# A decode attention kernel with one more key and one more value buffer, and with its last keys loaded ahead of the last values

## The chip, the cores and the metric

The kernel runs on one core of a Trainium2 chip. The metric is the device time of one execution in microseconds, median of several executions. Each kernel was also run once under the hardware profiler. The span of a profiled run, from first to last instruction, is 1.7 to 1.9 us shorter than the time taken of that same run.

## The reference, cut to what matters

Two decode attentions side by side, one query token and four batches each. A has 32 query heads on 8 key heads and looks at the last 2048 positions; B has 32 heads with a key cache of their own and 8192 positions.

```python
q = (x @ wq).reshape(B, 1, Hq, 128)
p = softmax(einsum("bhqd,bhkd->bhqk", q, k) * 128 ** -0.5)
out = einsum("bhqk,bhkd->bhqd", p, v).reshape(B, 1, Hq * 128) @ wo     # A and B concatenated
```

All in bfloat16. Keys and values are read once: 272 pieces of 2 MiB. With the weights that makes 587 MB.

## The kernel before

The work is cut into 136 chunks, 128 of B (one batch and head each) and then 8 of A (one key head, four batches each). A chunk has 64 blocks of 128 keys, taken in eight groups of eight. SyncE issues all loads in program order, and each waits only for the buffer that it overwrites:

```python
NKB = 3; NVB = 4; NPB = 3; SLAG = 2; PVLAG = 4; NG = 8          # buffers for K, V, P; lags in steps; groups
def dma_k(c):   # waits for the transposes of chunk c - NKB
    waits = [("T", (c - NKB + 1) * NG - 1)] if c >= NKB else []
def dma_v(c):   # waits for the values of chunk c - NVB
    waits = [("pv", c - NVB)] if c >= NVB else []
...
dma_x(1); dma_x(0); dma_wq(1); dma_k(0)
for c in range(NC):                      # load order
    if c + 1 < NC:
        dma_k(c + 1)
    dma_v(c)
    ...                                  # wq of A after c == 4, output weights when a chunk needs them
```

TensorE runs one static order, made of steps. In step s it transposes group s ("tr"), multiplies group s - 2 with the query ("sc"), and multiplies one group of an earlier chunk's values with its probabilities ("po"):

```python
for s in range(NC * NG):
    when(s, 0, lambda s=s: emit_T(s))                 # transposes; VectorE or ScalarE copies them out
    when(s + SLAG, 2, lambda s=s: emit_S(s))          # scores
for c in range(NC):
    s0 = c * NG + NG - 1 + SLAG
    when(s0, 3, ...stats_rowmax)                      # maximum: VectorE, TensorE (two small ones), VectorE
    when(s0 + 1, 1, ...stats_gmax)
    when(s0 + 2, 1, ...stats_exp)                     # exponentials on ScalarE, their sums on VectorE (A)
    for g in range(NG):
        when(s0 + PVLAG + g, 4, ...emit_pv)           # values
    if ch["ab"] == 0 or ch["b"] == NB - 1:
        when(s0 + PVLAG + 2, 1, ...norm_sum)          # TensorE adds the sums over the partitions
        when(s0 + PVLAG + NG - 1, 5, ...norm_out)     # VectorE divides: oT
        when(s0 + PVLAG + NG, 3, ...emit_fin)         # output projection: "fin"
```

In all timelines below an engine takes its instructions in this order, and where one waits, those behind it wait too.

Of the kernel before, what the change touches and what calls it, by code (L numbers as in the profile page):

```python
# [9 lines left out]
BF16 = mybir.dt.bfloat16  # L10
F32 = mybir.dt.float32

P = 128
TG = 8
NTRB = 3
NKT = 4
NKB = 3
NVB = 4
NWO = 4
NPB = 3  # L20
NSM = 4
SLAG = 2
NW = 64
PVLAG = 4
# [47 lines left out]
def bass_concat_heads__sliding_block_cached__mha_block_cached__decode_kernel(nc, A_x, A_k, A_v, A_wq, A_wo, B_x, B_k, B_v, B_wq, B_wo, out):  # L72
    NB = A_x.shape[0]
# [3 lines left out]
    HQ = A_wq.shape[1] // P  # L77
# [3 lines left out]
    KC = D // P  # L81
# [4 lines left out]
    NT = JB  # L86
    NG = NT // TG
    scale = 1.0 / math.sqrt(P)
    X = {0: A_x, 1: B_x}
    WQ = {0: A_wq, 1: B_wq}  # L90
# [8 lines left out]
    NC = len(chunks)  # L99
    wo_list = []  # L100
    for c, ch in enumerate(chunks):
# [3 lines left out]
        wo_list[-1][2] = c  # L105
        ch["wo_i"] = len(wo_list) - 1
    NBC = HB * NB

    sch = _Sched()
    with ExitStack() as es:  # L110
        block = es.enter_context(nc.Block())

        def sb(name, shape, dt):
            return es.enter_context(nc.sbuf_tensor(name, shape, dt))
# [3 lines left out]

        kn = sb("kn", [P, NKB, NT * P], BF16)
        vn = sb("vn", [P, NVB, NT * P], BF16)  # L120
        kt = sb("kt", [P, NKT, TG * P], BF16)
        wqr = sb("wqr", [P, KC * HQ * P], BF16)
        wor = sb("wor", [P, NWO, 4 * DO], BF16)
        xs = sb("xs", [NB, 2, D], BF16)
        xT = sb("xT", [P, 2, KC * NB], BF16)
# [12 lines left out]
        tmp = sb("tmp", [P, 2, 256], F32)  # L138
        pb = sb("pb", [P, NPB, 256 + NW], BF16)
        oT = sb("oT", [P, NSM, 16], BF16)  # L140
# [7 lines left out]

        semnames = ["eng_pe", "eng_dve", "eng_act", "eng_pool", "d_x0", "d_x1", "d_o0", "d_o1"]
        semnames += ["d_k%d" % i for i in range(NKB)] + ["d_v%d" % i for i in range(NVB)]  # L150
        semnames += ["d_wq%d" % i for i in range(2)] + ["d_wo%d" % i for i in range(NWO)]
        sems = {n: es.enter_context(nc.semaphore(n)) for n in semnames}


# [11 lines left out]


        def dma_x(ab):
            sch.add_dma("sp", lambda e: e.dma_start(xs[:, ab, :], X[ab][:, 0, :]), "d_x%d" % ab, key=("x", ab))

        def dma_wq(ab):

            n = KC // 2 * HQ * P
            for i in range(2):
                src = WQ[ab].rearrange("(p r) n -> p (r n)", r=KC)[:, i * n:(i + 1) * n]
                waits = [("qmm", 1)] if ab == 0 else []
                sch.add_dma("sp", lambda e, i=i, src=src: e.dma_start(wqr[:, i * n:(i + 1) * n], src),
                            "d_wq%d" % i, waits=waits, key=("wq", ab, i))

        def dma_wo(i):  # L180
            (ab, wg), _, _ = wo_list[i]
            slot = i % NWO
            src = WO[ab][wg * 4 * P:(wg + 1) * 4 * P, :].rearrange("(hl d) n -> d hl n", d=P)
            dst = wor[:, slot, :].rearrange("p (hl n) -> p hl n", hl=4)
            waits = [("fin", wo_list[i - NWO][2])] if i >= NWO else []
            sch.add_dma("sp", lambda e: e.dma_start(dst, src), "d_wo%d" % slot, waits=waits, key=("wo", i))

        def kv_src(T, ch):
            if ch["ab"] == 1:
                return T[ch["b"], ch["h"]].rearrange("(p j) d -> p (j d)", p=P)  # L190
            return T[:, ch["g"], SkA - W:, :].rearrange("b (p j) d -> p b (j d)", p=P)

        def kv_dst(buf, slot, ch):
            d = buf[:, slot, :]
            return d if ch["ab"] == 1 else d.rearrange("p (b x) -> p b x", b=NB)

        def dma_k(c):
            ch = chunks[c]
            src, dst = kv_src(A_k if ch["ab"] == 0 else B_k, ch), kv_dst(kn, c % NKB, ch)
            waits = [("T", (c - NKB + 1) * NG - 1)] if c >= NKB else []  # L200
            sch.add_dma("sp", lambda e: e.dma_start(dst, src), "d_k%d" % (c % NKB), waits=waits, key=("k", c))  # L201

        def dma_v(c):
            ch = chunks[c]
            src, dst = kv_src(A_v if ch["ab"] == 0 else B_v, ch), kv_dst(vn, c % NVB, ch)
            waits = [("pv", c - NVB)] if c >= NVB else []
            sch.add_dma("sp", lambda e: e.dma_start(dst, src), "d_v%d" % (c % NVB), waits=waits, key=("v", c))

        dma_x(1)
        dma_x(0)  # L210
        dma_wq(1)
        dma_k(0)
        wo_next = 0
        for c in range(NC):
            if c + 1 < NC:
                dma_k(c + 1)
            dma_v(c)
            if c == 4:
                dma_wq(0)
            while wo_next < len(wo_list) and wo_list[wo_next][1] <= c:  # L220
                dma_wo(wo_next)
                wo_next += 1


        ms_read = []
        po_read = []
# [14 lines left out]
        def emit_q(ab):  # L241
            for h in range(HQ):
                for r in range(KC):
                    o = ms[:, Q0 + h * NB: Q0 + (h + 1) * NB]
                    l = wqr[:, (r * HQ + h) * P:(r * HQ + h + 1) * P]
                    rr = xT[:, ab, r * NB:(r + 1) * NB]
                    last = h == HQ - 1 and r == KC - 1
                    sch.add("pe", lambda e, o=o, l=l, rr=rr, r=r: e.matmul(o, l, rr, start=(r == 0), stop=(r == KC - 1)),  # L248
                            waits=[("wq", ab, 0), ("wq", ab, 1), "xT"] + ([("q", 1)] if ab == 0 else []) + ms_read if h == r == 0 else [],
                            key=("qmm", ab) if last else None)  # L250
            src = ms[:, Q0:Q0 + HQ * NB].rearrange("p (h b) -> p h b", b=NB)
            dst = qs[:, ab * NB * HQ:(ab + 1) * NB * HQ].rearrange("p (b h) -> p h b", b=NB)
            sch.add("dve", lambda e: e.tensor_copy(dst, src), waits=[("qmm", ab), "c_qs"], key=("q", ab))
            ms_read[:] = [("q", ab)]


        def emit_T(s):
            c, g = divmod(s, NG)
            bank = s % NTRB
            for t in range(TG):  # L260
                o = tr[:, bank, t * P:(t + 1) * P]
                i_ = kn[:, c % NKB, (g * TG + t) * P:(g * TG + t + 1) * P]
                waits = []
# [59 lines left out]
        def stats_exp(c):  # L323
# [6 lines left out]
            ms_read[:] = [("negb", c)]  # L330
            pbv = pb[:, c % NPB, 0:NT * C]
            pw = [("pv", c - NPB)] if c >= NPB else []
            if n == 1:
# [29 lines left out]
        def emit_pv(c, g):  # L363
            ch = chunks[c]
            C, J = ch["C"], ch["J"]
            for t in range(TG):
                j = g * TG + t
                u, jj = divmod(j, J)
                base = norm_slot(c)[2] * 16 + (ch["b"] if ch["ab"] == 1 else u * C)
                o = po[:, base:base + NW]  # L370
                l = vn[:, c % NVB, j * P:(j + 1) * P]
                r = pb[:, c % NPB, j * C:j * C + NW]
                waits = [("v", c), "c_pb", ("exp", c)] + po_read if g == 0 and t == 0 else []
                sch.add("pe", lambda e, o=o, l=l, r=r, jj=jj: e.matmul(o, l, r, start=(jj == 0), stop=(jj == J - 1)),  # L374
                        waits=waits, key=("pv", c) if j == NT - 1 else None)

# [8 lines left out]
        def norm_out(c):  # L385
            m, n, s = norm_slot(c)
            sch.add("dve", lambda e: e.tensor_tensor(out=oT[:, m, 0:n], in0=po[:, s * 16:s * 16 + n], in1=rinv[:, m, 0:n], op=ALU.mult),  # L387
                    waits=[("rinv", c), ("pv", c)], key=("oT", c))
            po_read[:] = [("oT", c)]

        def emit_fin(c):
# [5 lines left out]
            else:  # L397
                ov = oT[:, m, 0:n].rearrange("p (u c) -> p u c", c=REP)
                ops = [(fin[32:32 + NB, :], ov[:, :, cc], w[:, cc, :]) for cc in range(REP)]
            lastc = NBC - 1 if ch["ab"] == 1 else NC - 1  # L400
            for i, (o, l, r) in enumerate(ops):
# [15 lines left out]
        def when(s, prio, fn):  # L417
            at.setdefault(s, []).append((prio, len(at.get(s, [])), fn))
# [4 lines left out]
        for c in range(NC):  # L423
            ch = chunks[c]
            s0 = c * NG + NG - 1 + SLAG
            when(s0, 3, lambda c=c: stats_rowmax(c))
            when(s0 + 1, 1, lambda c=c: stats_gmax(c))
            when(s0 + 2, 1, lambda c=c: stats_exp(c))
            for g in range(NG):
                when(s0 + PVLAG + g, 4, lambda c=c, g=g: emit_pv(c, g))  # L430
            if ch["ab"] == 0 or ch["b"] == NB - 1:
                when(s0 + PVLAG + 2, 1, lambda c=c: norm_sum(c))
                when(s0 + PVLAG + NG - 1, 5, lambda c=c: norm_out(c))
                when(s0 + PVLAG + NG, 3, lambda c=c: emit_fin(c))
        when(8 * NG, 5, lambda: emit_q(0))

        emit_xT()
        emit_q(1)
# [53 lines left out]
```

## Time and profile before

| | before |
|---|---|
| time, median of 3 | 1432.7 us (1432.53 to 1433.11) |
| span of the profiled run | 1431.4 us |
| TensorE busy, transfer engines busy | 83%, 9 tenths or more in 39 of 40 slices |
| last key chunk, last transfer, end | 1408.4, 1422.7, 1431.4 us |

The prediction below shows lines of the profile's page and reads them. Its times of landing do not stand on the page. The trace records sixteen semaphore updates for a transfer; "a chunk lands" means the sixteenth, and the spread is the time from the first to the sixteenth. The record of an update names no transfer engine. That each of the sixteen is one engine's, so that early and late updates are early and late engines, is the author's reading.

### The profile page before, as it was taken

Reading aid. Unit: us, or ns where it says so; the run is one execution under the profiler, and the core shown is the slowest. Engines: PE = TensorE matmul, PEld = TensorE weight load, DVE = VectorE, ACT = ScalarE, POOL = GpSimd, SP = SyncE. Lnnn points to the kernel's source line nnn. Section 1 sums busy time; section 2 is a strip of 40 time slices with the busy share of each in tenths; the row PEclk is TensorE's granted clock in tenths of the full one; section 3 lists DMA queues with packets and bytes.
Section 4 is the critical chain, followed back from the end, with each engine's and each line's share of the span. In section 5 each row is a group of like instructions: output and inputs, shape, how many; then the busy total and the mean of one; then the engine's idle time right before and its main releaser. Section 6 shows DMA issues by size and latency. Waiting matters only on the chain.

```text
span 1431.4 us, 56275 instructions
## 1 busy us (share of the span) xinstructions
PE 1195.2 (83%) x26928; PEld 1128.4 (79%) x26928; DVE 590.4 (41%) x1267; ACT 422.3 (30%) x627; POOL 2.4 (0%) x11
## 2 busy tenths in 40 slices
PE   5969888988888878888888888888888887888887
PEld 4858887887888877878778878787787787878776
DVE  2423443444444434444443434444434343444444
ACT  1312332332232322323323323333223232323221
POOL 0000000000000000000000000000000000000000
PEclk9988999999999999999999999999999999999999
DMA  9999999999999999999999999999999999999996
GB/s 389 425 426 426 425 422 422 426 424 424 423 422 424 422 422 420 410 422 416 423 412 424 416 419 407 424 418 421 423 407 425 419 418 415 419 418 406 370 395 244
DMA packets 54596, 590.83 MB, mean 413 GB/s; under 512 B 4688, under 2 KB 12896, under 8 KB 21088
## 3 DMA queue, kind: packets, MB, share of 16 engines
q1 hardware_dynamic: 54368, 587.24, 98.2%
q8 instruction: 211, 3.46, 1.0%
q14 instruction: 17, 0.14, 0.0%
HBM read 587.21 MB, written 0.01 MB: 410 GB/s over the span
## 4 chain that ended last, share of the span: by engine, by line
DMA 69%; PE 28%; issue 1%; DVE 1%; SPq 0%; ACT 0%; DVEq 0%
DMA kn<-in_B_k_cache_dram 56%; PE tr L266 13%; DMA vn<-in_B_v_cache_dram 8%; PE sc L295 7%; PE po L374 6%; DMA kn<-in_A_k_cache_dram 6%; PE ms L327 1%; PE ms L313 1%; PE fin L404 0%; PE ms L248 0%; DVE kt L273 0%; SPq L201 0%; PE ms L380 0%; DVE tmp L346 0%; DVE rm L307 0%
## 5 line engine op out<-in xcount | busy, mean ns | idle before, releaser
L266 PE MATMUL tr<-identb,kn 128*128 128x128 bf16 x8704 | 687.5, 223 | 196.1 <-DMA kn<-in_B_k_cache_dram 172.7
L273 DVE COPY kt<-tr 128x1024 bf16<-128x1024 bf16 x726 | 502.2, 692 | 714.2 <-PE tr L266 710.3
L266 PEld LDWEIGHTS tr<-identb,kn 128*128 128x128 bf16 x8704 | 520.0, 100 | 212.7 <-DMA kn<-in_B_k_cache_dram 186.1
L271 ACT ACTIVATE kt<-tr 128x1024 bf16<-128x1024 bf16 x362 | 370.7, 1024 | 857.2 <-PE tr L266 851.6
L295 PE MATMUL sc<-qs,kt 128*128 128x64 bf16 x8704 | 452.3, 195 | 7.3 <-issue 7.2
L374 PE MATMUL po<-pb,vn 128*128 128x64 bf16 x8704 | 449.4, 195 | 9.9 <-issue 7.4
L295 PEld LDWEIGHTS sc<-qs,kt 128*128 128x128 bf16 x8704 | 376.8, 100 | 13.4 <-issue 9.0
L374 PEld LDWEIGHTS po<-pb,vn 128*128 128x128 bf16 x8704 | 342.3, 99 | 22.9 <-issue 18.4
L335 ACT ACTIVATE pb<-sc,negb 128x64 bf16<-128x64 f32 x128 | 40.0, 312 | 126.2 <-DVE negb L329 126.2
L327 PE MATMUL ms<-gm,nsc 1*128 1x1 f32 x256 | 48.5, 256 | 0.8 <-issue 0.8
L327 PEld LDWEIGHTS ms<-gm,nsc 1*128 1x128 f32 x256 | 37.7, 183 | 13.6 <-issue 0.2
L315 DVE TENSOR_REDUCE gm<-ms 1x1 f32<-1x128 f32 (+1 forms) x136 | 37.0, 272 | 20.2 <-PE ms L313 20.2
L307 DVE TENSOR_REDUCE rm<-sc 128x1 f32<-128x64 f32 (+1 forms) x136 | 31.3, 230 | 29.7 <-PE sc L295 29.4
L313 PE MATMUL ms<-identf,rm 128*1 128x128 f32 (+1 forms) x136 | 38.3, 282 | 1.3 <-DVE rm L307 1.3
L329 DVE COPY negb<-ms 128x1 f32<-128x1 f32 (+1 forms) x136 | 20.8, 153 | 27.8 <-PE ms L327 27.8
L335 ACT ACTIVATION_READ_ACCUMULATOR pb<-sc,negb 128x1 f32 x128 | 25.1, 196 | 0.0
L404 PE MATMUL fin<-wor,oT 128*4 128x512 bf16 x64 | 20.3, 378 | 4.1 <-DVE oT L387 4.1
L313 PEld LDWEIGHTS ms<-identf,rm 128*1 128x1 f32 (+1 forms) x136 | 11.5, 85 | 13.5 <-DVE rm L307 13.4
L248 PE MATMUL ms<-xT,wqr 128*128 128x4 bf16 x256 | 7.0, 166 | 10.9 <-DMA wqr<-in_B_wq_dram 10.9
L248 PEld LDWEIGHTS ms<-xT,wqr 128*128 128x128 bf16 x256 | 6.9, 102 | 10.9 <-issue 10.9
L380 PE MATMUL ms<-rs,onesf 128*128 128x4 f32 (+1 forms) x80 | 13.6, 241 | 0.0
L380 PEld LDWEIGHTS ms<-rs,onesf 128*128 128x128 f32 x80 | 12.1, 191 | 0.0
(26 smaller groups left out, 45.3 us busy)
## 6 DMA issues: line engine op xcount, KB each, us to landing
kn<-in_B_k_cache_dram SPq DMA_DIRECT2D x128, 2048.0 KB, 22.5
vn<-in_B_v_cache_dram SPq DMA_DIRECT2D x128, 2048.0 KB, 27.1
kn<-in_A_k_cache_dram SPq DMA_DIRECT2D x8, 2048.0 KB, 21.3
vn<-in_A_v_cache_dram SPq DMA_DIRECT2D x8, 2048.0 KB, 21.5
wqr<-in_B_wq_dram SPq DMA_DIRECT2D x2, 2048.0 KB, 9.6
wor<-in_B_wo_dram SPq DMA_DIRECT2D x8, 512.0 KB, 28.1
wqr<-in_A_wq_dram SPq DMA_DIRECT2D x2, 2048.0 KB, 32.8
wor<-in_A_wo_dram SPq DMA_DIRECT2D x8, 512.0 KB, 17.4
```

What stands on the lines that cost most here:

```text
L266: sch.add("pe", lambda e, o=o, i_=i_: e.transpose(o, i_, identb[:, :]), waits=waits, key=("T", s) if t == TG - 1 else None)
L271: sch.add("act", lambda e: e.activation(dst, src, ACTF.Copy), waits=waits, key=("ev", s))
L273: sch.add("dve", lambda e: e.tensor_copy(dst, src), waits=waits, key=("ev", s))
L295: sch.add("pe", lambda e, o=o, l=l, q=q: e.matmul(o, l, q, start=True, stop=True), waits=waits, key=("S", s) if t == TG - 1 else None)
L307: sch.add("dve", lambda e: e.tensor_reduce(out=dst, in_=src, axis=AX.X, op=ALU.max), waits=[("S", (c + 1) * NG - 1)], key=("rowmax", c))
L313: sch.add("pe", lambda e: e.transpose(ms[0:n, col:col + P], rm[:, m, 0:n], identf[:, :]), waits=[("rowmax", c), "c_identf"] + ms_read, key ...
L315: sch.add("dve", lambda e: e.tensor_reduce(out=gm[0:n, m, :], in_=ms[0:n, col:col + P], axis=AX.X, op=ALU.max), waits=[("trm", c)], key=(" ...
L327: sch.add("pe", lambda e: e.matmul(ms[:, col:col + n], nsc[0:n, :], rhs, start=True, stop=True), waits=[("dg", c) if n > 1 else ("gmax", c ...
L329: sch.add("dve", lambda e: e.tensor_copy(negb[:, m, 0:n], ms[:, col:col + n]), waits=[("bc", c)], key=("negb", c))
L335: sch.add("act", lambda e: e.activation(pbv, sc[:, c % 2, 0:NT], ACTF.Exp, bias=negb[:, m, 0:1], scale=scale, accum_out=ri), waits=[("negb ...
L374: sch.add("pe", lambda e, o=o, l=l, r=r, jj=jj: e.matmul(o, l, r, start=(jj == 0), stop=(jj == J - 1)), waits=waits, key=("pv", c) if j == ...
L380: sch.add("pe", lambda e: e.matmul(ms[:, col:col + n], onesf[:, :], rs[:, m, 0:n], start=True, stop=True), waits=[("rs", c), "c_onesf"] + ...
```

## The change

Its intent: keep more transfers under way, and end the kernel with less work behind the last transfer. The query weights, 32 KB a partition, now lie in value buffers that are not yet in use, and the room pays for one more buffer each for keys and values. All keys are loaded ahead of the last three value chunks (133, 134, 135), so that only values are left to do when the last bytes land, and the last value chunk comes as four transfers, each with its own semaphore. The core of the diff:

```diff
-NKB = 3
-NVB = 4
+NKB = 4
+NVB = 5
-NPB = 3
+NPB = 4
-        wqr = sb("wqr", [P, KC * HQ * P], BF16)
+        wqr = {1: vn[:, 0:2, :].rearrange("p s x -> p (s x)"), 0: vn[:, 2:4, :].rearrange("p s x -> p (s x)")}
@@ x loads: issued by ScalarE instead of SyncE
-            sch.add_dma("sp", ... xs[:, ab, :] ...)
+            sch.add_dma("act", ... xs[:, ab, :] ...)
@@ dma_v
-            waits = [("pv", c - NVB)] if c >= NVB else []
+            waits = [("pv", c - NVB)] if c >= NVB else ([("qmm", 1 - slot // 2)] if slot < 4 else [])
+            if c == NC - 1:
+                for u in range(NB):
+                    sch.add_dma("sp", ... dst[:, u, :], src[:, u, :] ..., "d_vl%d" % u, ...)
+                return
@@ load order
+        loads = [("k", c + 1) for c in range(NC - 1)]
+        for c in range(NC):
+            loads.insert(min(2 * c + 1, NC - 1 + c) if c < NC - 3 else len(loads), ("v", c))
@@ order of TensorE
+            v0 = s0 + PVLAG if c < NC - 3 else (NC - 1) * NG + NG - 1 + SLAG + PVLAG + (c - NC + 1) * NG + 2 * NG
-                when(s0 + PVLAG + g, 4, lambda c=c, g=g: emit_pv(c, g))
+                when(v0 + g, 4, lambda c=c, g=g: emit_pv(c, g))
-                when(s0 + PVLAG + NG - 1, 5, lambda c=c: norm_out(c))
-                when(s0 + PVLAG + NG, 3, lambda c=c: emit_fin(c))
+                when(v0 + NG - 1, 5, lambda c=c: norm_out(c))
+                when(v0 + NG, 3, lambda c=c: emit_fin(c))
```

(A's query weights are loaded at the start, the second query matmuls move from step 64 to step 5, and output weights are loaded one chunk earlier.) The values of chunks 133, 134 and 135 now follow, one after the other, all transposes and scores.

More of the change, by code (lines that the diff above doesn't have):

```diff
@@ L107, in bass_concat_heads__sliding_block_cached__mha_block_cached__decode_kernel @@
     NBC = HB * NB
+    assert KC * HQ == 2 * NT
     sch = _Sched()
@@ L150, in bass_concat_heads__sliding_block_cached__mha_block_cached__decode_kernel @@
         semnames += ["d_k%d" % i for i in range(NKB)] + ["d_v%d" % i for i in range(NVB)]
-        semnames += ["d_wq%d" % i for i in range(2)] + ["d_wo%d" % i for i in range(NWO)]
+        semnames += ["d_wq0", "d_wq1"] + ["d_vl%d" % i for i in range(NB)] + ["d_wo%d" % i for i in range(NWO)]
         sems = {n: es.enter_context(nc.semaphore(n)) for n in semnames}
@@ L168, in dma_x @@
         def dma_x(ab):
-            sch.add_dma("sp", lambda e: e.dma_start(xs[:, ab, :], X[ab][:, 0, :]), "d_x%d" % ab, key=("x", ab))
+            sch.add_dma("act", lambda e: e.dma_start(xs[:, ab, :], X[ab][:, 0, :]), "d_x%d" % ab, key=("x", ab))
+        wqr = {1: vn[:, 0:2, :].rearrange("p s x -> p (s x)"), 0: vn[:, 2:4, :].rearrange("p s x -> p (s x)")}
         def dma_wq(ab):
-            n = KC // 2 * HQ * P
-            for i in range(2):
-                src = WQ[ab].rearrange("(p r) n -> p (r n)", r=KC)[:, i * n:(i + 1) * n]
-                waits = [("qmm", 1)] if ab == 0 else []
-                sch.add_dma("sp", lambda e, i=i, src=src: e.dma_start(wqr[:, i * n:(i + 1) * n], src),
-                            "d_wq%d" % i, waits=waits, key=("wq", ab, i))
+            src = WQ[ab].rearrange("(p r) n -> p (r n)", r=KC)
+            sch.add_dma("sp", lambda e: e.dma_start(wqr[ab], src), "d_wq%d" % ab, key=("wq", ab))
         def dma_wo(i):
@@ L204, in dma_v @@
             ch = chunks[c]
-            src, dst = kv_src(A_v if ch["ab"] == 0 else B_v, ch), kv_dst(vn, c % NVB, ch)
-            waits = [("pv", c - NVB)] if c >= NVB else []
-            sch.add_dma("sp", lambda e: e.dma_start(dst, src), "d_v%d" % (c % NVB), waits=waits, key=("v", c))
+            slot = c % NVB
+            src, dst = kv_src(A_v if ch["ab"] == 0 else B_v, ch), kv_dst(vn, slot, ch)
+            waits = [("pv", c - NVB)] if c >= NVB else ([("qmm", 1 - slot // 2)] if slot < 4 else [])
+            if c == NC - 1:
+                for u in range(NB):
+                    sch.add_dma("sp", lambda e, u=u: e.dma_start(dst[:, u, :], src[:, u, :]), "d_vl%d" % u, waits=waits, key=("vl", u))
+                return
+            sch.add_dma("sp", lambda e: e.dma_start(dst, src), "d_v%d" % slot, waits=waits, key=("v", c))
         dma_x(1)
@@ L212, in bass_concat_heads__sliding_block_cached__mha_block_cached__decode_kernel @@
         dma_k(0)
+        dma_wq(0)
+        loads = [("k", c + 1) for c in range(NC - 1)]
+        for c in range(NC):
+            loads.insert(min(2 * c + 1, NC - 1 + c) if c < NC - 3 else len(loads), ("v", c))
         wo_next = 0
-        for c in range(NC):
-            if c + 1 < NC:
-                dma_k(c + 1)
-            dma_v(c)
-            if c == 4:
-                dma_wq(0)
-            while wo_next < len(wo_list) and wo_list[wo_next][1] <= c:
-                dma_wo(wo_next)
-                wo_next += 1
+        for kind, c in loads:
+            (dma_k if kind == "k" else dma_v)(c)
+            if kind == "v":
+                while wo_next < len(wo_list) and wo_list[wo_next][1] <= c + 1:
+                    dma_wo(wo_next)
+                    wo_next += 1
         ms_read = []
@@ L244, in emit_q @@
                     o = ms[:, Q0 + h * NB: Q0 + (h + 1) * NB]
-                    l = wqr[:, (r * HQ + h) * P:(r * HQ + h + 1) * P]
+                    l = wqr[ab][:, (r * HQ + h) * P:(r * HQ + h + 1) * P]
                     rr = xT[:, ab, r * NB:(r + 1) * NB]
@@ L248, in emit_q @@
                     sch.add("pe", lambda e, o=o, l=l, rr=rr, r=r: e.matmul(o, l, rr, start=(r == 0), stop=(r == KC - 1)),
-                            waits=[("wq", ab, 0), ("wq", ab, 1), "xT"] + ([("q", 1)] if ab == 0 else []) + ms_read if h == r == 0 else [],
+                            waits=[("wq", ab), "xT"] + ([("q", 1)] if ab == 0 else []) + ms_read if h == r == 0 else [],
                             key=("qmm", ab) if last else None)
@@ L372, in emit_pv @@
                 r = pb[:, c % NPB, j * C:j * C + NW]
-                waits = [("v", c), "c_pb", ("exp", c)] + po_read if g == 0 and t == 0 else []
+                waits = ["c_pb", ("exp", c)] + po_read if g == 0 and t == 0 else []
+                if c == NC - 1:
+                    waits += [("vl", u)] if jj == 0 else []
+                elif j == 0:
+                    waits += [("v", c)]
                 sch.add("pe", lambda e, o=o, l=l, r=r, jj=jj: e.matmul(o, l, r, start=(jj == 0), stop=(jj == J - 1)),
@@ L428, in bass_concat_heads__sliding_block_cached__mha_block_cached__decode_kernel @@
             when(s0 + 2, 1, lambda c=c: stats_exp(c))
+            v0 = s0 + PVLAG if c < NC - 3 else (NC - 1) * NG + NG - 1 + SLAG + PVLAG + (c - NC + 1) * NG + 2 * NG
             for g in range(NG):
-                when(s0 + PVLAG + g, 4, lambda c=c, g=g: emit_pv(c, g))
+                when(v0 + g, 4, lambda c=c, g=g: emit_pv(c, g))
             if ch["ab"] == 0 or ch["b"] == NB - 1:
                 when(s0 + PVLAG + 2, 1, lambda c=c: norm_sum(c))
-                when(s0 + PVLAG + NG - 1, 5, lambda c=c: norm_out(c))
-                when(s0 + PVLAG + NG, 3, lambda c=c: emit_fin(c))
-        when(8 * NG, 5, lambda: emit_q(0))
+                when(v0 + NG - 1, 5, lambda c=c: norm_out(c))
+                when(v0 + NG, 3, lambda c=c: emit_fin(c))
+        when(5, 5, lambda: emit_q(0))
         emit_xT()
```

## The prediction

Its sum came to 1429.6 us for the span and 1430.9 for the time. What the trace of before does show: after 460 us the largest gap among a transfer's sixteen updates lies behind the eighth, in all 172 transfers of B; and the clock is at half in 21 stretches of 3.4 to 13.7 us, the last from 1409.3 for 3.4, behind the wait of 2.14 us for key 135. That the 24 long steps are the fetches of q8, and that eight engines share these, is an estimate from the page's count and share.

> **What bounds the kernel now.** I read the page's DMA part first, then the chain of waits, then the single transfers' landings, and last the TensorE timeline of the final 35 us.
>
> ```profile
> DMA  9999999999999999999999999999999999999996
> GB/s 389 425 426 426 425 422 422 426 424 424 423 422 424 422 422 420 410 422 416 423 412 424 416 419 407 424 418 421 423 407 425 419 418 415 419 418 406 370 395 244
> ...
> q1 hardware_dynamic: 54368, 587.24, 98.2%
> q8 instruction: 211, 3.46, 1.0%
> ...
> DMA 69%; PE 28%; issue 1%; DVE 1%; SPq 0%; ACT 0%; DVEq 0%
> ```
>
> The transfer engines are busy in every slice but the last, and the chain that ended last is 69% transfers: the kernel streams 587 MB and TensorE (83% busy[...]) follows. The change moves the same bytes, so the first question is whether the 410, 407 and 370 GB/s slices are lost time that more buffers could win back.
>
> They look like it. In this view of two stretches (busy times of the engines, then the granted clock, the DMA share and GB/s) a hole can be seen:
>
> ```profile
> 573.00:577.00 4.00, 4.00 (x108) 4.00 (x104) 1.98 (x3) 1.02 (x1) 0.00 (x0) 1.00 0.74 291
> 577.00:584.00 7.00, 6.08 (x145) 5.66 (x142) 3.35 (x8) 2.45 (x4) 0.00 (x0) 1.00 0.99 412
> ```
>
> But the trace also records each of the sixteen semaphore updates of every transfer[...]. Sorted by time they say something else. The spread from first to last of the sixteen is 0.5 us for the first keys (18.2 to 18.7 us), 8 us near 270 us, 14 us near 450 us, and then stays at 14 to 16 us to the end of the B stage. Always about eight engines are early and eight late. And the last of the sixteen lands at 574.6, 579.6, 584.4, 589.3, 594.2 us straight across the hole: a step of 4.9 us for each 2 MiB, as in the fullest slices. **The late engines never pause; only the early ones do**, because they have used up all that the buffers let be issued. Of the 253 steps of the last update between 50 and 1305 us, nearly all are 4.9 us (or 1.5 for an output-weight load), and 24 are 6.4 us. The q8 row explains those 24: 211 instruction fetches, 1.0% of 16 engines' 1431 us, so 1.1 us each; 211 over eight engines is 26 each. The slowest engine therefore needs 246 steps of 4.89 us, 7 of 1.5 and 24 extras of 1.5, together 1250 us, and took 1251. It has no idle time to give back.
>
> Now the end. Rows are start, duration, engine, line, operation, and in brackets the idle time and its releaser:
>
> ```profile
> 1385.06 0.62 PE L266 MATMUL tr<-identb,kn 128*128 128x128 bf16 x8 [1.29 <-DMA kn<-in_A_k_cache_dram]
> ...
> 1396.76 0.62 PE L266 MATMUL tr<-identb,kn 128*128 128x128 bf16 x8 [1.65 <-DMA kn<-in_A_k_cache_dram]
> ...
> 1408.44 0.62 PE L266 MATMUL tr<-identb,kn 128*128 128x128 bf16 x8 [2.14 <-DMA kn<-in_A_k_cache_dram]
> ...
> 1422.11 0.39 PE L327 MATMUL ms<-dg,nsc 16*128 16x16 f32 x2 [0.40 <-DVE dg L319]
> 1422.43 0.64 PE L374 MATMUL po<-pb,vn 128*128 128x64 bf16 x16
> 1424.40 1.03 PE L404 MATMUL fin<-wor,oT 128*4 128x512 bf16 x4 [1.33 <-DVE oT L387]
> ...
> 1427.96 1.03 PE L404 MATMUL fin<-wor,oT 128*4 128x512 bf16 x4 [0.34 <-DVE oT L387]
> ```
>
> The last three key chunks (133, 134, 135) arrive at 1385.0, 1396.7 and 1408.4. The last value chunk has landed at 1421.4 and the last output weights at 1422.7 (sixteenth updates), yet the span ends at 1431.4: from 1408.4 on it is a TensorE chain of 23.0 us, which outlives the last transfer by 8.7 us.
>
> [...] the x loads moved to ScalarE's queue are worth what they held up: the first weight load is issued at 1.53 us, behind two x issues that start at 0.81. [...] the clock is 0.79 in 1408 to 1416.
>
> **The change part by part.**
>
> 1. Query weights in the value buffers. 32 KB a partition come free and pay for one more K and one more V buffer of 16 KB. New waits: V0 and V1 wait for the first query matmuls (done near 18 us), V2 and V3 for the second. Issued ahead of those are 4+2+4+2 MiB, which at 424 GB/s keep the engines busy to some 32 us, and then K2, K3, V0, V1 to some 50 us. The second query matmuls wait for weights landing near 29 us, so they end near 34 us: no hole. Cost 0.
>
> 2. One more buffer each. The early eight engines may run some 10 us further ahead; the late eight gain nothing, by the working above. Worth 0. The holes should shrink all the same.
>
> 3. x on the other queue: everything lands 1.53 - 0.81 = 0.7 us earlier. NPB 4 changes nothing: its wait is on work long done.
>
> 4. Keys ahead. Each output-weight load goes one chunk earlier. Key 134 comes after the same bytes as before plus one such load (1.45 us) minus 0.7: 1396.7 + 0.75 = 1397.5. Key 135 follows 5.1 us later, at 1402.6, not at 1408.4. All loads still end near 1422.7 - 0.7 = 1422.0, now with the last V piece.
>
> TensorE from there, every piece from the rows of before: chunk 134's eight groups took 9.4 us warm (1396.76 to 1406.2) with eight value groups of 0.235 us in between; three of these leave for later, so 8.7, to 1406.2. Then chunk 135 at once, without any value groups (8 x 0.235) and without an output projection (0.96): 9.4 - 2.84 = 6.6, so 1412.8. Its last score matmuls start 1.57 us after the last transposes' start (1418.72 to 1420.29), thus near 1413.9; 1.8 us on (to 1422.11) comes the broadcast of the maximum, 1415.7, and 0.32 later the postponed values of chunk 133, at 1416.05. After two of their groups stands the sum over chunk 135's exponentials, in program order, and those are ready 2.16 us after the broadcast (1422.11 to 1424.27): **a new wait of about 1.4 us**, to 1417.9. Sum 0.2, six groups 1.4, normalization gap 0.32: projection of 133 at 1419.9. Then twice (0.96 projection, 1.88 values, 0.32 gap): projection of 134 at 1423.05, of 135 at 1426.2. From there to the end it was 1431.38 - 1427.96 = 3.42 us. End: 1429.6, that is 1.8 us less. The last V piece (1422.0) is there before TensorE comes to chunk 135's values (1424.0), so cutting it in pieces is worth nothing yet.
>
> The timed figure is 1.3 us above the profiled span (1432.7 against 1431.4): 1430.9.
>
> **The rivals.**
>
> - The end is set by the last transfer: TensorE catches up. Then 1422.0 + 16 matmuls (0.5) + 0.3 + 3.42 = 1426.2, timed 1427.5. For it: the diff is built for this. Against: the sum above, 3.4 us longer.
> - The stream itself gets faster through the buffers. At 426 GB/s throughout, 590.8 MB need 1387 us, the end would be near 1400, 2% less. For it: the holes. Against: the unbroken 4.9 us steps of the sixteenth updates.
> - A cold clock in the new tail. Waiting for key 134 (some 1.7 us) or in the new 1.4 us wait the clock may halve for 3 to 4 us: plus 1.5 to 2, so 1432.7, no gain. For it: 0.79 in 1408 to 1416 before. Against: chunk 135 now follows 134 without a wait.
> - A fetch falls late on the slowest engine: plus or minus 1.5 us on the last landings, hidden where TensorE is the bound.
>
> **Range and chances.** Some 0.55 for the main sum (1430.9), 0.25 for something near the transfer bound (1428), 0.15 for the cold clock (1432.7), little for the stream. Mean 1430.4, said as 1430.5; range 1427.3 to 1433.0. Two per cent is 28.7 us, over three times all that lies after the last landing (8.7), so only the stream rival could reach it: 0.02 faster, 0.01 slower.
>
> **What would show it.** Sixteenth updates in B still 4.9 us apart with some 24 long steps, their spread growing to some 25 us: step 2 right. Key 135 landing near 1402.6, last landing near 1422.0: step 4. TensorE waiting for ScalarE's or VectorE's sum of chunk 135 near 1417, no wait on V pieces, end near 1429.6: the tail. The prediction is wrong if the last landing moves by more than 3 us, or if TensorE waits for the last V piece.

## The result, and the profile after

The changed kernel took **1434.15 us** (1433.66 to 1434.8, 4 runs); the kernel before, in the same rounds, 1432.89. The ratio is 1.0009, with a 95% interval of 0.9992 to 1.0027: the same. A ratio here and below is the mean time of one kernel's runs over the mean of the other's of the same rounds, so not quite the ratio of the medians quoted. The prediction was 1430.5, and 1434.15 lies above its range (to 1433.0). The profiled run took 1434.55, with a span of 1432.8.

The page of the changed kernel, the lines that answer to those shown of before (the share of transfers in the chain last):

```profile
DMA  9999999999999999999999999999999999998995
GB/s 401 422 425 424 424 423 425 424 427 420 425 424 425 424 423 424 426 425 422 422 426 424 408 416 423 425 424 393 423 426 422 414 411 426 422 419 345 367 398 223
...
q1 hardware_dynamic: 54112, 587.23, 97.9%
q8 instruction: 211, 3.46, 1.0%
...
DMA 79%; PE 19%; DVE 1%; issue 0%; SPq 0%; ACT 0%; DVEq 0%
```

The stream as a whole has not moved: the same 587 MB and the same 211 instruction fetches; slices 37 and 38, where A begins, are at 345 and 367 GB/s, for 406 and 370 before. Yet the buffers do what they were made for. From the list of transfers, with the size of one and the median time from issue to landing, first of before, then of the changed kernel:

```profile
kn<-in_B_k_cache_dram SPq DMA_DIRECT2D x128, 2048.0 KB, 22.5
vn<-in_B_v_cache_dram SPq DMA_DIRECT2D x128, 2048.0 KB, 27.1
```

```profile
kn<-in_B_k_cache_dram SPq DMA_DIRECT2D x128, 2048.0 KB, 32.4
vn<-in_B_v_cache_dram SPq DMA_DIRECT2D x128, 2048.0 KB, 36.9
```

Each chunk is asked for 10 us earlier and lands when it did. For the end, the TensorE timeline of the changed kernel from the maximum of chunk 135 on (L320 and L334), to be compared with the last rows of before in the prediction:

```profile
1415.39 0.28 PE L320 MATMUL ms<-identf,rm 128*16 128x128 f32 x1 [0.52 <-DVE rm L314]
1416.30 0.39 PE L334 MATMUL ms<-dg,nsc 16*128 16x16 f32 x2 [0.63 <-DVE dg L326]
1416.62 0.80 PE L385 MATMUL po<-pb,vn 128*128 128x64 bf16 x16
1418.51 0.61 PE L391 MATMUL ms<-rs,onesf 128*128 128x16 f32 x2 [1.09 <-DVE rs L360]
1418.96 2.72 PE L385 MATMUL po<-pb,vn 128*128 128x64 bf16 x48
1421.95 1.87 PE L415 MATMUL fin<-wor,oT 128*4 128x512 bf16 x4 [0.27 <-DVE oT L398]
1423.75 2.04 PE L385 MATMUL po<-pb,vn 128*128 128x64 bf16 x64
1426.06 1.03 PE L415 MATMUL fin<-wor,oT 128*4 128x512 bf16 x4 [0.27 <-DVE oT L398]
1427.01 2.04 PE L385 MATMUL po<-pb,vn 128*128 128x64 bf16 x64
1429.39 1.03 PE L415 MATMUL fin<-wor,oT 128*4 128x512 bf16 x4 [0.34 <-DVE oT L398]
```

The wait of 1.09 us for the sum of chunk 135 (L391) is new. The values of chunk 135 start at 1427.01, with no transfer in the brackets: the last of them had landed at 1422.2, so the four pieces were of no use. And the same work takes two different times: 48 value matmuls take 2.72 us at 1418.96, where before they took 1.56, and four projections 1.87 us at 1421.95, but 1.03 at 1426.06. The row of before:

```profile
1426.06 1.56 PE L374 MATMUL po<-pb,vn 128*128 128x64 bf16 x48
```

That is the clock. Stretches of the changed kernel's run (busy time of each engine with its count, then the granted clock, the DMA share, GB/s):

```profile
1406.00:1414.00 8.00, 7.03 (x149) 6.52 (x147) 5.98 (x17) 3.42 (x4) 0.00 (x0) 1.00 1.01 386
1414.00:1418.00 4.00, 2.15 (x39) 1.53 (x35) 2.29 (x10) 0.41 (x1) 0.00 (x0) 0.87 0.52 204
1418.00:1424.00 6.00, 5.22 (x63) 3.61 (x64) 0.85 (x3) 0.00 (x1) 0.00 (x0) 0.52 0.18 74
1424.00:1432.80 8.80, 5.81 (x134) 4.11 (x130) 1.03 (x3) 0.00 (x0) 0.00 (x0) 1.00 0.01 2
```

TensorE is busy for only 2.15 of the 4 us from 1414 on, and has half its clock, by the trace's record, from 1416.9 for 6.8 us.

Step by step, by the prediction's own list:

| | predicted us | measured us |
|---|---|---|
| spread of the sixteen updates, end of B | some 25 | 22.6 to 24.2 |
| key 134, key 135 land | 1397.5, 1402.6 | 1397.7, 1402.8 |
| last transfer lands | 1422.0 | 1422.2 |
| transposes of 135 begin | 1406.2 | 1406.4 |
| values of 133 begin | 1416.05 | 1416.6 |
| new wait for the sum ends | 1417.9 | 1418.5 |
| projection of 133 | 1419.9 | 1421.95 |
| projection of 134 | 1423.05 | 1426.06 |
| projection of 135 | 1426.2 | 1429.39 |
| end | 1429.6 | 1432.8 |

### The profile page after: what moved, and what is told of

It is laid out like the page before. It is cut to its first block, busy times and chain, and to the rows that moved or that the text cites. A ratio compares the mean times of both kernels' runs of the same rounds, so it can differ in the third digit from the quotient of the medians. Undisturbed runs are those within 1.5% of the kernel's fastest.

```text
span 1432.8 us, 56273 instructions
## 1 busy us (share of the span) xinstructions
PE 1203.7 (84%) x26928; PEld 1133.7 (79%) x26928; DVE 590.2 (41%) x1267; ACT 421.8 (29%) x627; POOL 2.7 (0%) x11
## 4 chain that ended last, share of the span: by engine, by line
DMA 79%; PE 19%; DVE 1%; issue 0%; SPq 0%; ACT 0%; DVEq 0%
DMA kn<-in_B_k_cache_dram 66%; PE tr L273 9%; DMA kn<-in_A_k_cache_dram 7%; DMA vn<-in_B_v_cache_dram 5%; PE po L385 4%; PE sc L302 4%; DMA vn<-in_A_wq_dram 2%; PE ms L334 1%; PE ms L320 0%; DVE kt L280 0%; PE fin L415 0%; PE ms L255 0%; PE ms L391 0%; DVE rm L314 0%; DVE tmp L353 0%
## 5 line engine op out<-in xcount | busy, mean ns | idle before, releaser
L334 PE MATMUL ms<-gm,nsc 1*128 1x1 f32 x256 | 48.5, 256 | 0.5 <-issue 0.4
L334 PEld LDWEIGHTS ms<-gm,nsc 1*128 1x128 f32 x256 | 37.5, 182 | 14.1 <-issue 0.5
L320 PE MATMUL ms<-identf,rm 128*1 128x128 f32 (+1 forms) x136 | 38.4, 282 | 1.6 <-DVE rm L314 1.6
L320 PEld LDWEIGHTS ms<-identf,rm 128*1 128x1 f32 (+1 forms) x136 | 11.6, 85 | 13.5 <-DVE rm L314 13.4
L255 PE MATMUL ms<-xT,vn 128*128 128x4 bf16 x256 | 7.1, 166 | 10.4 <-DMA vn<-in_A_wq_dram 6.0
L398 DVE TENSOR_TENSOR oT<-po,rinv 128x4 bf16<-128x4 f32 (+1 forms) x40 | 6.3, 158 | 21.9 <-PE po L385 21.9
L255 PEld LDWEIGHTS ms<-xT,vn 128*128 128x128 bf16 x256 | 7.0, 104 | 10.6 <-DMA vn<-in_A_wq_dram 6.1
L391 PE MATMUL ms<-rs,onesf 128*128 128x4 f32 (+1 forms) x80 | 13.8, 244 | 1.1 <-DVE rs L360 1.1
```

The source lines that it names most:

```text
L320: sch.add("pe", lambda e: e.transpose(ms[0:n, col:col + P], rm[:, m, 0:n], identf[:, :]), waits=[("rowmax", c), "c_identf"] + ms_read, key ...
L334: sch.add("pe", lambda e: e.matmul(ms[:, col:col + n], nsc[0:n, :], rhs, start=True, stop=True), waits=[("dg", c) if n > 1 else ("gmax", c ...
```

## The experiments

**Theory.** The stream ends when its slowest transfer engine does, and the buffers can't hurry that engine. The tail after the last key is one chain on TensorE. The change cut the wait for keys from it but laid the values of three chunks behind it, and made pauses (0.52, 0.63 and 1.09 us), around which the clock fell to half for 6.8 us. **Rivals.** Either deeper buffers do win time in the stream and the tail loses it again; or the last transfer sets the end, and no order on TensorE matters. Four runs come first.

### Only the buffers

Buffers, query weights and x loads as in the change; load order, TensorE order and whole last values as before.

```diff
-            loads.insert(min(2 * c + 1, NC - 1 + c) if c < NC - 3 else len(loads), ("v", c))
+            loads.insert(min(2 * c + 1, NC - 1 + c), ("v", c))
-            v0 = s0 + PVLAG if c < NC - 3 else (NC - 1) * NG + NG - 1 + SLAG + PVLAG + (c - NC + 1) * NG + 2 * NG
+            v0 = s0 + PVLAG
```

> Only the new buffers (query weights in the value buffers, 4 K, 5 V, 4 P buffers, x on the other queue); load order, value groups and whole last V as before the change. Theory (the eight late transfer engines never pause, buffers win nothing): 1432.2 us, the 0.7 us of the earlier start and no more; sixteenth landings in B still 1251 us for the same 253 steps. Rival (the holes in the DMA rate were lost time that deeper buffers win back): 1405 to 1428 us.

Measured: 1432.3 us (1431.44 to 1432.94, 5 runs) beside 1432.53; ratio 0.9997 (0.9983 to 1.001). The 253 steps of the sixteenth update in B took 1250.8 us, against 1251.2 before, while the median key landed 32.5 us after its issue instead of 22.5. The rival that buffers win time in the stream falls. Whether the 0.7 us of the start are there can't be told from times that scatter by 1.5 us; the last landing is at 1421.7 instead of 1422.7.

### The sum later

```diff
-                when(s0 + PVLAG + 2, 1, lambda c=c: norm_sum(c))
+                when(s0 + PVLAG + 2 if c < NC - 1 else v0 + 2, 1, lambda c=c: norm_sum(c))
```

> The changed kernel with the sum over chunk 135's exponentials moved from between the values of chunk 133 to after two groups of chunk 135's values. Theory (the tail is one TensorE chain, lengthened by the 1.1 us wait for this sum and by the half clock that follows the pauses): 1.1 us less for the wait, 1433.0, and some 2.5 us less again if the clock stays full because TensorE no longer pauses, 1430.5. Rival (the last transfer sets the end): 1434.1, no change.

Measured: 1430.68 us (1430.16 to 1432.56, 5 runs); ratio to before 0.9988 (0.9976 to 1.0001). The last transfer lands at 1422.1, as in the changed kernel, and every run is faster than every run of the changed kernel, so the rival that it sets the end falls. The clock did fall, at 1417.4, but for 3.4 us instead of 6.8. The profiled span was 1430.8, 2.0 us less than the changed kernel's: more than the wait alone (1.1), less than wait and clock together.

### Transposes that nobody reads, in the pauses

Eight before L320, ten before L334, sixteen before L391 (`e0` is the step of chunk 135's maximum):

```diff
+        def fill(n):
+            for i in range(n):
+                o = tr[:, 2, (i % TG) * P:(i % TG + 1) * P]
+                sch.add("pe", lambda e, o=o: e.transpose(o, identb[:, :], identb[:, :]), waits=[("ev", NC * NG - 3)])
+        when(e0 + 1, 0, lambda: fill(8)); when(e0 + 2, 0, lambda: fill(10)); when(e0 + PVLAG + 2, 0, lambda: fill(16))
```

> The changed kernel with 34 transposes of the identity, whose result nobody reads, put where TensorE waits in the tail (8 before the transposed maximum, 10 before the broadcast, 16 before the sum). No wait is removed. Theory (the half clock from 1417 to 1424 us costs 2.6 us and comes of the pauses): the clock stays full, 1431.5. Rival (the clock is not what costs, or it falls for another reason): 1434 or a little more.

Measured: 1432.12 us (1431.63 to 1434.55, 5 runs); ratio to before 0.9999 (0.9986 to 1.0011). The TensorE timeline of this run (L451 are the added ones):

```profile
1414.97 0.61 PE L451 MATMUL tr<-identb 128*128 128x128 bf16 x8
...
1417.36 1.06 PE L451 MATMUL tr<-identb 128*128 128x128 bf16 x16
1418.77 0.40 PE L391 MATMUL ms<-rs,onesf 128*128 128x16 f32 x2 [0.35 <-DVE rs L360]
1419.01 1.56 PE L385 MATMUL po<-pb,vn 128*128 128x64 bf16 x48
1420.84 1.03 PE L415 MATMUL fin<-wor,oT 128*4 128x512 bf16 x4 [0.27 <-DVE oT L398]
```

The sum comes no earlier (1418.77 against 1418.51), but the 48 value matmuls take 1.56 us instead of 2.72 and the projections 1.03 instead of 1.87. Adding useless work took about 2 us off this tail. From the start of the broadcast (L334) to the end it is 14.3 us here. In the four profiles of the tail without these transposes it is 16.5, 16.7 and 16.8 us where the clock was halved for 6.8 us (the changed kernel, and the runs with one whole last value chunk and with eight engines, below), and 15.7 where it was halved for 3.4 (the changed kernel again, below). By the medians the gain is of that size too, but their intervals overlap; the profiles are what shows it.

When did the clock fall? In the records of before and of the changed kernel every stretch within the span, at full clock or at half, lasts 3.41 us or a multiple of it, up to 13.65 at half clock. Windows here are these 3.4 us. TensorE's busy time in the window ahead of the fall was 2.1 us in the changed kernel and 2.1 in the run with the later sum; with the added transposes it was 3.1 in the same stretch, and the clock stayed. In none of these does TensorE pause for more than 0.63 us at once. But busy time does not tell the cases apart: in the run with the buffers alone TensorE is busy for 2.1 us of the window from 1421.6 too, and the clock stays full. What does is the number of columns that the matmuls which start in the window stream (128 for a transpose, 64 for a score or value matmul, 512 for a projection): 2416 in the changed kernel and 2720 with the later sum, against 4736 with the transposes and 3744 with the buffers alone. Counted over all 14 profiles, from 41 us on and without the last windows of each, 5347 windows had the full clock and 315 of them were followed by half of it. None of the 315 had more than 3200 columns, and none of the others fewer than 2888. Of the windows with 1.5 to 2.14 us of busy time, 26 were followed by a fall and 615 were not.

### The values of chunk 133 between

If pauses cost, useful work belongs in them. The values of 133 have landed at 1407.9, and the transposes of 135 begin at 1406.4.

```diff
-            v0 = s0 + PVLAG if c < NC - 3 else (NC - 1) * NG + NG - 1 + SLAG + PVLAG + (c - NC + 1) * NG + 2 * NG
+            v0 = s0 + PVLAG if c < NC - 3 else (NC - 1) * NG + 4 + (c - NC + 3) * NG
```

(The sum of 135 as in "The sum later".)

> The changed kernel with the values of chunk 133 put between the last transposes and scores of chunk 135 and into its waits, 134 and 135 directly after, and the sum of 135 inside its own values. Theory (the end is a TensorE chain whose waits can hold work): about 4 us off the chain, with a full clock a span near 1427.5, timed 1429; the last V piece (1422.2) just begins to matter. Rival (the last transfer sets the end): no change, 1434.

Measured: 1431.95 us (1430.74 to 1432.99, 5 runs); ratio 0.9994 (0.9981 to 1.0006). A miss, and the timeline shows why:

```profile
1416.68 0.41 PE L385 MATMUL po<-pb,vn 128*128 128x64 bf16 x8
1418.64 1.87 PE L415 MATMUL fin<-wor,oT 128*4 128x512 bf16 x4 [1.56 <-DVE oT L398]
```

The projection of 133 waits 1.56 us for its normalization (oT), although the values of 133 are done at 1417.1. The last group of those values stands in the same step as the statistics of 135, so VectorE has the sum over 135's exponentials in its queue first, and that waits for ScalarE. The clock fell again, from 1418.1 for 3.4 us.

### One step earlier

```diff
-            v0 = s0 + PVLAG if c < NC - 3 else (NC - 1) * NG + 4 + (c - NC + 3) * NG
+            v0 = s0 + PVLAG if c < NC - 3 else (NC - 1) * NG + 3 + (c - NC + 3) * NG
```

In VectorE's order the division for 133 now comes ahead of the statistics of 135. This run was sent with three others; first the changed kernel again, unaltered, then the same with one whole last value chunk.

> The changed kernel unaltered, on the chip of this job, to see how far two runs of one kernel differ. Theory (its tail ends about 10.5 us after the last landing, whether or not a half-clock window of 3.4 or 6.8 us falls on it): 1431 to 1435 us, last landing near 1422.2. Rival (it is truly slower than before in some other place): the last landing later than before's 1422.7.

```diff
-            if c == NC - 1:
+            if False:                                         # the last value chunk loaded whole
-                if c == NC - 1:
-                    waits += [("vl", u)] if jj == 0 else []
-                elif j == 0:
+                if j == 0:                                    # and waited for whole
                     waits += [("v", c)]
```

> The changed kernel with the last value chunk loaded whole and waited for whole. Theory (the last V has landed before TensorE comes to it): the same as the changed kernel beside it within 1 us, and no wait on a V transfer in the tail. Rival (the pieces let TensorE start on the last V early): 1.4 us more, and TensorE waits for V.

> The values of chunk 133 one step earlier than in the run values_between, so that VectorE's normalization of 133 stands before the exponential statistics of 135 in its queue; the rest as there. Theory (in values_between the projection of 133 waited 1.56 us because its normalization stood behind ScalarE's exponentials in VectorE's order): that wait goes, values of 135 start near 1420.8, ahead of the last V piece at 1422.1, and the last transfer sets the end: span 1426.5 to 1427.5, timed 1428 to 1429. Rival (another wait takes its place): span 1430, timed 1431.5.

Measured beside 1432.7 for the kernel before:

| | time us | range (5 runs) | ratio to before, 95% | span of the profiled run |
|---|---|---|---|---|
| changed, again | 1434.4 | 1433.39 to 1436.16 | 1.0012 (1.0000 to 1.0024) | 1431.6 |
| one whole last V | 1434.93 | 1433.62 to 1434.97 | 1.0013 (1.0001 to 1.0024) | 1433.2 |
| values one step earlier | 1429.46 | 1428.54 to 1430.32 | 0.9976 (0.9964 to 0.9988) | 1426.7 |

The changed kernel repeats, and its clock falls again in both profiles of the first two rows (at 1417.8 for 3.4 us, at 1417.6 for 6.8), which would account for most of the 1.6 us between their spans. In pieces or whole makes no difference to it. The third beats the kernel before, by 0.24%, and the changed one. Its timeline:

```profile
1416.16 0.39 PE L334 MATMUL ms<-dg,nsc 16*128 16x16 f32 x2 [0.40 <-DVE dg L326]
1416.48 1.03 PE L415 MATMUL fin<-wor,oT 128*4 128x512 bf16 x4
1417.44 2.04 PE L385 MATMUL po<-pb,vn 128*128 128x64 bf16 x64
1419.74 1.03 PE L415 MATMUL fin<-wor,oT 128*4 128x512 bf16 x4 [0.27 <-DVE oT L398]
1420.70 0.64 PE L385 MATMUL po<-pb,vn 128*128 128x64 bf16 x16
1421.18 0.37 PE L391 MATMUL ms<-rs,onesf 128*128 128x16 f32 x2
1421.40 1.56 PE L385 MATMUL po<-pb,vn 128*128 128x64 bf16 x48
1423.30 1.03 PE L415 MATMUL fin<-wor,oT 128*4 128x512 bf16 x4 [0.34 <-DVE oT L398]
```

The broadcast of the maximum (L334) is where it was in the changed kernel, 1416.2 against 1416.3. But the projection of 133 follows at once, and the projection of 135 starts 6.1 us earlier. All at full clock: 4896 columns in the 3.4 us from 1413.6. The last landing is 1421.8 and the end 4.9 us later. But no line waits for a value transfer: TensorE comes to the last piece, the last 16 of these 64 value matmuls, at 1422.3, 0.5 us after it landed. So even here the last transfer does not set the end: that part of the expectation did not come true, though little is missing.

### The last value chunk, where TensorE arrives early

```diff
-            if c == NC - 1:
-                for u in range(NB): ...
+            # the last value chunk as any other, in the kernel "values one step earlier"
```

> The kernel of values_earlier with the last value chunk in one piece. Theory (there TensorE comes to the last values at 1420.7, before the last landing at 1421.8, so here the pieces do count): TensorE waits for V some 1.1 us, values of 135 from 1422.0, span 1427.8 against 1426.7, timed 1 us more than values_earlier. Rival (pieces are worth nothing here either): the same time.

Measured: 1430.19 us (1429.88 to 1431.39, 5 runs), ratio to before 0.9984 (0.9972 to 0.9997), span 1428.1. The line that decides:

```profile
1422.12 0.63 PE L383 MATMUL po<-pb,vn 128*128 128x64 bf16 x16 [0.26 <-DMA vn<-in_A_v_cache_dram]
```

Now TensorE waits for values. The wait is only 0.26 us because in this run the projection of 134 came 1.1 us later (1420.84 against 1419.74). So the span is 1.4 us longer than with pieces, but this trace puts down only that wait to the missing pieces; the rest came earlier in the run, and the profiled run with pieces was the fastest of its five. By the ratios the pieces are worth 1.1 us, with overlapping intervals.

### Transposes that nobody reads, in the best kernel

```diff
+        when(e0 + 1, 0, lambda: fill(5)); when(e0 + 2, 0, lambda: fill(6))      # fill as above
```

> The kernel of values_earlier with 11 transposes of the identity, read by nobody, in the two pauses before chunk 135's maximum. Theory (in values_earlier the clock was full through the tail already): no change in the profiled run, 1429.5, and a narrower scatter if the clock fell in some of its unprofiled runs. Rival (the clock falls in many runs): up to 1.5 us less.

Measured: 1429.38 us (1428.68 to 1430.17, 5 runs), ratio 0.9977 (0.9965 to 0.999), clock full through the tail. No change, as expected: there was no fall left to prevent.

### What sets the stream

> The kernel of the run values_earlier plus 12288 one-element memsets on GpSimd, which has nothing else to do after 4 us. They move no data through the transfer queues but are 64 bytes each to fetch, 0.79 MB or 48 fetches of 16 KB more than the 211. Theory (instruction fetches delay eight of the sixteen transfer engines by 1.5 us each, and the slowest engine sets the stream): 6 more per late engine, last landing 9 us later, near 1431, time near 1438.5. Rival (fetches fill holes of the queue, or land on early engines): 1429.5, no change.

```diff
+        for i in range(NJUNK):                                # 12288
+            sch.add("pool", lambda e, i=i: e.memset(junk[:, i:i + 1], 0.0))
```

Measured: 1464.36 us (1463.5 to 1465.62, 4 runs), ratio to before 1.0221 (1.0207 to 1.0235). In direction right, in size wrong: about 35 us more than without the memsets (1429.46) instead of 9. Two lines of the page of this run:

```profile
q8 instruction: 211, 3.46, 0.9%
q14 instruction: 113, 0.93, 0.2%
```

GpSimd's fetches do not come on q8 but on q14 (17 packets without them), 96 more packets of 8 KB, which is 64 bytes for each memset. And of the sixteen updates of each transfer near 300 us, fifteen now come within 3 us, and **one** comes about 30 us after the first. The last landing moved from 1421.8 to 1455.7 us, 33.9 us, which is 0.35 us for each of the 96. By the author's reading one transfer engine carried them all, and the other fifteen could not go on, for the buffers allow no larger lead; the records do not name it. From 180 to 500 us the best kernel has a DMA share of 1.01 at 424 GB/s, this one 0.94 at 376. First the best kernel, then this one:

```profile
180.00:500.00 320.00, 269.03 (x6174) 254.85 (x6170) 132.90 (x279) 97.69 (x148) 0.00 (x0) 0.98 1.01 424
```

```profile
180.00:500.00 320.00, 257.72 (x5504) 246.20 (x5501) 118.55 (x248) 86.83 (x134) 260.09 (x7791) 0.91 0.94 376
```

The memsets did not slow VectorE: its busy time is 0.478 us an instruction with them and 0.476 without. This supports the main point about buffers. Here a delay of one update out of sixteen, with fetches that move 0.1% of the bytes, came with a last landing 33.9 us later. What one more buffer of each kind changed in the stream is how early a chunk is asked for (by 10 us) and the spread: 22.6 to 24.2 us from 1200 us to the end of B, where before it was 13.0 to 16.0; the 253 steps took 1250.9 us, before 1251.2.

Could bytes be moved from the late engines to the early ones? Two runs tried it by loading four key chunks as sixteen transfers of 8 partitions. In the trace of the first, 144 updates belong to the first split chunk: 16 come while the transfers are issued (155.2 to 160.3 us) and 128, eight for each transfer, from 176.8 us on. That such a load runs on eight engines is read from this; which eight they are no run here shows. What both expectations said of that is cut, and with it the conditions of their estimates, four steps of 4.9 us either way: if the eight were early ones, about 1415 us for the first run (the figure left standing below) and 1412 for the second; if they were late ones, about 1453 and 1449.

> The changed kernel with four of the 136 key chunks loaded as sixteen transfers of 8 partitions each[...]. Theory (eight late engines set the stream, eight early ones wait): [...] the late engines save 4 x 4.9 us and the last landing moves from 1422 to about 1403 and the time to about 1415[...]. Rival (all engines share the bound, the spread is harmless): no gain, a few us more for smaller transfers.

```diff
+            if c in (16, 48, 80, 112):
+                for i in range(16):
+                    r = slice(8 * i, 8 * i + 8)
+                    sch.add_dma("sp", ... dst[r, :], src[r, :] ...)
```

> As eight_engines, on the kernel of values_earlier, but each of the sixteen small transfers of a key chunk takes 8 partitions that lie 4 apart instead of 8 neighbours. Theory (in eight_engines the small transfers were slow for their 8 neighbouring partitions, not for the eight engines): the 20 us holes around the split chunks shrink or vanish. [...] Rival (any transfer of 8 partitions is that slow): some 1510 again.

```diff
-                    r = slice(8 * i, 8 * i + 8)
+                    r = slice(32 * (i // 4) + i % 4, 32 * (i // 4) + i % 4 + 29, 4)
```

Measured: 1519.84 us (1515.02 to 1529.16) with neighbouring partitions, on the changed kernel, and 1482.53 (1480.23 to 1484.62) with spread ones, on the best kernel: 85 and 53 us more than those kernels. Each split chunk leaves a hole; with neighbouring partitions the stretch from 160 to 215 us, around the first, moves 294 GB/s, the next 55 us 425. With spread partitions the loss was thus 32 us smaller. The first is far above every number expected of it, the second lies between the 1449 and the 1510 expected, and the cost of these small transfers hides what was asked. **Inconclusive**: which engines are the late ones, and whether they could be relieved, stays open.

## Why the prediction was wrong

**What bounds the kernel: right.** The prediction held that the late engines never pause and that buffers are worth 0. The changed kernel needs 1250.9 us for the 253 steps, before 1251.2, and the run with buffers alone shows no gain. The fetches as the cause of the lateness were argued from counts; the run with more fetches shows, for 96 more of them, one update of sixteen some 30 us late and the last landing 33.9 us later. That the 211 fetches of q8 fall on eight engines is still an inference, and the sizes do not quite match: by the q8 row a fetch takes 1.1 us, but a long step is 1.5 us longer. A small misreading: the spread of before did not stay at 14 to 16 us, it moved between 12.3 and 16.0.

**Buffers, start, keys: right.** Every landing in the table is within 0.2 us. That it is so close is partly luck: in the other profiles with this load order, those with split chunks or more fetches left out, key 135 lands between 1402.3 and 1403.2.

**The new wait: right.** It was to end at 1417.9 and ended at 1418.5. It measured 1.09 us, against about 1.4.

**The step that failed** is the sum from there on, which took every piece from rows at full clock, together with the weight of the rival "A cold clock in the new tail", 0.15, with "Against: chunk 135 now follows 134 without a wait". That argument looked at the wait for a key. What the clock followed in these traces is how many columns TensorE streamed within 3.4 us, and with the pauses for the maximum and the broadcast (0.52 and 0.63 us) only 2416 were left in the window from 1413.5, where with 4736 it stayed full. The fall came at 1416.9, ahead of the new wait of 1.09 us; that wait lies in the next window, after which the clock stayed halved. It fell in all four profiles taken of this tail. (The tail of before has its own 3.4 us of half clock, from 1409.3, behind a wait of 2.14 us for key 135; the change took that away and put its own in place.) Of the 3.2 us between 1429.6 and 1432.8, 0.6 had come by the end of the new wait, 2.3 come at half clock up to the values of 134 (a sum and six value groups with their gap in 3.44 us instead of 2.0, a projection in 1.80 instead of 0.96), and 0.3 are value groups slightly longer than taken. With the clock held up by useless transposes the span was 1430.9, so a fault of about 1.3 us would have remained at full clock: partly the later start, partly those transposes.

**A second, smaller fault**: 1.3 us were added to get from span to time, by setting a median of three runs against the span of another run. The profiled run itself had taken 1433.19, so the right figure was 1.8. Altogether 1430.9 + 3.2 + 0.45 - 0.4 = 1434.15, where 0.4 is what the profiled run lies above its median. The answer given, 1430.5, lay 0.4 lower for the faster rivals.

**The rivals.** "The end is set by the last transfer" got 1426.2 for the span; the version with values one step earlier ends at 1426.7, though TensorE waits for no value transfer there. The load order of the change was good for that much. Its order on TensorE gave it away: before, key 135 landed at 1408.4 and 23.0 us followed; after, at 1402.8 and 30.0 followed. Keys came 5.6 us earlier, and the tail grew by 7.0.

## What to carry to other kernels

In a kernel like this one, look at the sixteen updates of a transfer, not at the mean rate: here slices of 410, 407 and 370 GB/s looked like lost time, and more buffers won none of it (1432.3 us beside 1432.53). Moving loads ahead at the end of the kernel paid nothing (1434.15 beside 1432.89) until the postponed work stood in the waits of the last statistics, and in the right order on VectorE too (1431.95, then 1429.46 one step earlier). And count the columns that TensorE streams in the last microseconds: here the clock halved after 3.4 us with 2416 columns and pauses of at most 0.63 us, and stayed full with 4736.
